# Batch 0 of a Fourier-filter and MLP kernel: one spectrum for both filter products, a second inverse table for the factor i, angles by integer shifts, input DMAs first

## Chip, cores, metric

One core of a Trainium2 chip. The metric is the device time of one execution in microseconds (us). Most executions of one kernel agree within 0.3%. Every quoted ratio is the mean time of one kernel's fast runs over that of the kernel before in the same rounds on the same chip, so it is not quite the ratio of the medians quoted beside it; the brackets hold a 95% interval. Medians of different kernels come from different rounds and chips; so where a gain in us is given, it is the excess of a median over that of the kernel before in the same rounds.

## The reference, cut to what matters

```python
# x: (8, 3008, 256), filt_r and filt_i: (1505, 256), w_in: (256, 2048), w_out: (2048, 256)
X = np.fft.rfft(x, axis=1)
Y = X * (filt_r + 1j * filt_i)[None]
y = np.fft.irfft(Y, n=3008, axis=1).reshape(24064, 256)
h = y @ w_in
return (0.5 * h * (1 + erf(h / sqrt(2)))) @ w_out
```

## The kernel before

The transforms are matmuls with tables of sines. Batch 0 goes first, alone; the MLP follows, with batches 1 to 7 woven between its matmuls. Only batch 0's prologue matters here. A filter product (`c2`) multiplies the spectrum by `filt_r` and by `filt_i`. The second product needs the spectrum turned by i, so PE computes it twice, from a table `T2` that holds three forms of each row side by side (turned with a minus, plain, turned):

```python
# c2: filter product p of 12 (two of 24 frequency rows)
for t, o in ((0, 1), (1, 0)):
    for i in range(2):
        k = 2 * p + i
        nc.tensor.matmul(ps[:, t, 256 * i:256 * i + 256],
                         lhsT=self.T2[:, k, o:o + 2].rearrange("p a b -> p (a b)"),
                         rhs=self.st[0, "b", k // 4][:, k % 4, :], start=True, stop=True)
f = self.F[:, :, 2 * p:2 * p + 2, :]
nc.vector.tensor_tensor(out=w, in0=ps, in1=f.rearrange("p t a b -> p t (a b)"), op=ALU.mult)   # VectorE
# c3: inverse transform; t = 0 and t = 1 add up in PSUM, both with the same table
nc.tensor.matmul(ps[half][:, c:c + 128], lhsT=w[:, t, o:o + 128],
                 rhs=self.T3[:, 2 * (p + i) + k]..., start=t == 0, stop=t == 1)
```

The filter `F` is loaded to partitions 0 to 63 and must also stand in 64 to 127. The order of what touches it (cuts marked):

```python
m.load_x(0, 1, 4)                                      # x: casting DMAs from GpSimd
...
for k, n in ((0, 4), (4, 4), (8, 8), (16, 8)):
    m.load_filters(k, n)                               # 16 casting DMAs from GpSimd
m.dup_filters(nc.gpsimd, 4, 4)                         # copies to partitions 64 to 127, two rows each
m.load_w_in()
m.dup_filters(nc.gpsimd, 8, 8)
...                                                    # column transforms c1, c1t
m.dup_filters(nc.vector, 0, 4)
...
m.dup_filters(nc.gpsimd, 16, 8)
m.load_x(1); m.load_w_out(0); m.load_w_out(8)
m.c2(0); m.c2(1)
...                                                    # q = 1 to 6: c2, c1t, c3; table_4 at q = 4
# the tail: c3t (transposes) and c4 (last transform), then the MLP with batch 1's first step s1 in slot 1
```

Of the kernel before, what the change touches and what calls it, by code (L numbers as in the profile page):

```python
# [21 lines left out]
TCH = 512  # L22

# [5 lines left out]
class _Mix:  # L29
    def __init__(self, ctx, tc, x, filt_r, filt_i, w_in, w_out, out):  # L30
# [23 lines left out]
        self.T2 = c.tile([128, K1, 3, NB], BF16, name="T2")  # L54
# [42 lines left out]

    def gate(self, t):

        g = self.po.tile([1, 1], BF16, tag="gate", name="gate")  # L100
        self.nc.gpsimd.tensor_copy(out=g, in_=t)  # L101
# [22 lines left out]
    def table_1(self, g):  # L124
# [3 lines left out]
        k48 = self.iota(g, "k48", [128, 2, K1], [[0, 2], [1, K1]])  # L128
        off = g.tile([128, 2, K1], FP32, name="off")
        nc.gpsimd.memset(off[:, 0, :], 0.25)  # L130
        nc.gpsimd.memset(off[:, 1, :], 0.5)
# [7 lines left out]
        nc.vector.scalar_tensor_tensor(out=w, in0=k48, scalar=n1, in1=off, op0=ALU.mult, op1=ALU.add)  # L139
# [6 lines left out]
    def table_2(self, g):  # L146
# [8 lines left out]
        self.n2, ri = col("n2"), col("ri")  # L155
        v.tensor_copy(out=self.n2, in_=m_i)
        v.tensor_copy(out=ri, in_=ri_i)
        ts(out=self.n2, in0=self.n2, scalar1=1.0 / self.S, scalar2=None, op0=ALU.mult)
        ts(out=ri, in0=ri, scalar1=-0.25, scalar2=0.25, op0=ALU.mult, op1=ALU.add)
        self.jn = g.tile([128, NB], FP32, name="jn")  # L160
        ts(out=self.jn, in0=self.jj, scalar1=self.n2, scalar2=ri, op0=ALU.mult, op1=ALU.add)
        self.n12, self.sg, self.to = col("n12"), col("sg"), col("to")
        ts(out=self.n12, in0=self.n2, scalar1=float(K1 // 2), scalar2=None, op0=ALU.mult)

        ts(out=self.sg, in0=ri, scalar1=8.0, scalar2=-1.0, op0=ALU.mult, op1=ALU.add)
        v.tensor_tensor(out=self.to, in0=self.p, in1=self.sg, op=ALU.add)

    def unit_matrices(self, g, cols):
        ts = self.nc.vector.tensor_scalar
        self.eye, self.swap = (g.tile([128, 128], BF16, name=n) for n in ("eye", "swap"))  # L170
        ts(out=self.eye, in0=cols, scalar1=self.p, scalar2=None, op0=ALU.is_equal)
        ts(out=self.swap, in0=cols, scalar1=self.to, scalar2=self.sg, op0=ALU.is_equal, op1=ALU.mult)

    def table_2_angle(self, h):

        v, k = self.nc.vector, K1 // 2
        w, r = self.gen[:, h], self.gen[:, 2]
        if h == 0:
            v.scalar_tensor_tensor(out=w, in0=self.kk.unsqueeze(2).to_broadcast([128, k, NB]), scalar=self.n2,
                                   in1=self.jn.unsqueeze(1).to_broadcast([128, k, NB]), op0=ALU.mult, op1=ALU.add)  # L180
        else:
            v.tensor_scalar(out=w, in0=self.gen[:, 0], scalar1=self.n12, scalar2=None, op0=ALU.add)
        v.tensor_scalar(out=r, in0=w, scalar1=RND, scalar2=-RND, op0=ALU.add, op1=ALU.add)
        v.tensor_tensor(out=w, in0=w, in1=r, op=ALU.subtract)

    def table_2_sin(self, h):
        self.nc.scalar.activation(out=self.T2[:, 12 * h:12 * h + 12, 1, :], in_=self.gen[:, h], func=AF.Sin,
                                  scale=2.0 * PI)

    def table_2_swap(self, h):  # L190
        t2 = self.T2[:, 12 * h:12 * h + 12]
        for i in range(2):
            ps = self.bank("ps_sw", "n")
            self.nc.tensor.matmul(ps[:, 0:384], lhsT=self.swap, rhs=t2[:, :, 1, 32 * i:32 * i + 32],
                                  start=True, stop=True)
            self._evac(t2[:, :, 2, 32 * i:32 * i + 32], ps[:, 0:384].rearrange("p (k j) -> p k j", k=12),
                       "act", 1.0 - 2.0 * i)
            if h == 1:
                self._evac(t2[:, :, 0, 32 * i:32 * i + 32], ps[:, 0:384].rearrange("p (k j) -> p k j", k=12),
                           "act", 2.0 * i - 1.0)  # L200

    def table_2_minus(self):
        t2 = self.T2[:, 0:12]
        self.nc.vector.tensor_scalar(out=t2[:, :, 0, :], in0=t2[:, :, 2, :], scalar1=-1.0, scalar2=None, op0=ALU.mult)
# [22 lines left out]
    def table_3(self, q, eng):  # L227
        ps = self.bank("ps_t3", "n", BF16)
        for i in range(8):
            self.nc.tensor.transpose(ps[:, 128 * i:128 * i + 128],  # L230
                                     self.T2[:, 8 * q + i, 1:3].rearrange("p a b -> p (a b)"), self.eye)

        self._evac(self.T3[:, 8 * q:8 * q + 8], ps.rearrange("p (k n r) -> p k r n", k=8, r=2), eng)

    def warm_up(self, n):

        ps = self.bank("ps_warm", "w")
        for i in range(n):
            self.nc.tensor.matmul(ps[:, i % 2], lhsT=self.ones[:, 0:128], rhs=self.ones, start=True, stop=True)
# [50 lines left out]
    def s2(self, b, p):  # L290
        nc = self.nc
        ps = self.bank("ps_s2")
        for i in range(2):
            k = 2 * p + i
            nc.tensor.matmul(ps[:, 256 * i:256 * i + 256], lhsT=self.T2[:, k, 1:3].rearrange("p a b -> p (a b)"),  # L295
# [70 lines left out]
    def c1t(self, q, eng):  # L366
# [6 lines left out]
        self._evac(b[:, 0:4, :].rearrange("p a b -> p (a b)"), ps, eng)  # L373

    def c2(self, p):
# [4 lines left out]
        for t, o in ((0, 1), (1, 0)):  # L380
            for i in range(2):
                k = 2 * p + i
                nc.tensor.matmul(ps[:, t, 256 * i:256 * i + 256],
                                 lhsT=self.T2[:, k, o:o + 2].rearrange("p a b -> p (a b)"),
                                 rhs=self.st[0, "b", k // 4][:, k % 4, :], start=True, stop=True)
# [121 lines left out]
def kernel(  # L507
# [50 lines left out]
    for u in range(16):  # L558
# [9 lines left out]
        if u == 11:  # L568
            m.warm_up(2)
# [115 lines left out]
```

## Time and profile before

The median is 774.5 us. The stages, from the busy time by stage that the prediction quotes (span 772.2 us):

| stage | us | what sets it |
|---|---|---|
| loads of x and filter, tables, column transforms | 0 to 16.72 | the load of x |
| 12 filter products | 16.72 to 32.02 | VectorE, then GpSimd's copies of F |
| tail: inverse transform to y | 32.02 to 40.55 | VectorE's copies and ACT's evictions in turn |
| first MLP tile, with batch 1's first step | 40.55 to 50.92 | PE, busy 10.33 of 10.37 us |
| the rest | 721.28 long | PE, busy 718.32 us |

### The profile page before, as it was taken

To read this page: it belongs to the slowest core of one execution; us is meant where nothing else is said; L and a number is where in the kernel's file an instruction comes from. 1 tells how busy PE (TensorE), PEld (TensorE's weight loads), DVE (VectorE), ACT (ScalarE), POOL (GpSimd) and SP (SyncE) were. 2 spreads that over 40 slices of the span, in tenths; PEclk is the share of its full clock that TensorE was granted. 3 is DMA by queue.
4 is the path that set the end of the run, shared out by engine and by line. 5 is a ranking of instruction groups with operands and counts; after the bars stand their busy time and mean duration, and the time that the engine had idled before them with its cause. 6 is when DMAs were issued, how large, how long until landed. Compare 5 with 4: busy or idle time off the path is not lost.

```text
span 772.2 us, 15059 instructions
## 1 busy us (share of the span) xinstructions
PE 763.2 (99%) x6066; PEld 528.7 (68%) x6066; DVE 397.3 (51%) x722; ACT 567.4 (73%) x981; POOL 64.9 (8%) x160
## 2 busy tenths in 40 slices
PE   8999999999999999999999999999999999999998
PEld 4847675676776766677777776666776776766666
DVE  7866755464555645457463664637646366411011
ACT  6879955897568975699656996579865798666663
POOL 7801100020000200011000110001100000000000
PEclk9999999999999999999999999999999999999999
DMA  8894745466253661636516464255553422410111
GB/s 138 145 180 124 150 123 129 128 124 151 57 139 107 138 159 41 192 78 122 143 53 181 85 133 123 79 154 95 124 137 81 139 83 69 123 42 28 42 42 55
DMA packets 87398, 85.66 MB, mean 111 GB/s; under 512 B 6752, under 2 KB 77536, under 8 KB 87328
## 3 DMA queue, kind: packets, MB, share of 16 engines
q1 hardware_dynamic: 78816, 68.70, 31.0%
q0 software_dynamic: 8512, 16.00, 14.9%
q8 instruction: 47, 0.77, 0.4%
q14 instruction: 23, 0.19, 0.1%
HBM read 54.00 MB, written 46.66 MB: 130 GB/s over the span
## 4 chain that ended last, share of the span: by engine, by line
PE 94%; DMA 3%; POOL 2%; issue 0%; DVE 0%; POOLq 0%
PE ps_o L488 43%; PE ps_h L461 42%; PE ps_s L345 2%; PE ps_s L320 2%; PE ps_s L295 2%; PE ps_s L272 2%; DMA x_sb<-in_x_dram 2%; POOL F L96 1%; POOL x_sb L82 1%; DMA F<-in_filt_i_dram 1%; POOL F L91 0%; PE ps_e L478 0%; POOL T1s L258 0%; DVE ost L501 0%; POOL T1p L580 0%
## 5 line engine op out<-in xcount | busy, mean ns | idle before, releaser
L464 ACT ACTIVATE g_sb<-ps_h 128x512 bf16<-128x512 f32 x752 | 438.0, 597 | 182.8 <-PE ps_h L461 172.1
L488 PE MATMUL ps_o<-w_out_sb,g_sb 128*128 128x256 bf16 x2992 | 447.5, 273 | 0.0
L461 PE MATMUL ps_h<-y_sb,w_in_sb 128*128 128x512 bf16 (+3 forms) x1600 | 445.8, 366 | 0.7 <-DMA x_sb<-in_x_dram 0.7
L488 PEld LDWEIGHTS <-g_sb 128*128 128x128 bf16 x2992 | 283.9, 98 | 134.3 <-issue 9.9
L461 PEld LDWEIGHTS <-w_in_sb 128*128 128x128 bf16 x1600 | 154.7, 98 | 23.7 <-issue 1.1
L494 DVE COPY ost<-ps_o 128x512 f32<-128x512 f32 x93 | 63.8, 686 | 143.5 <-PE ps_o L488 143.4
L303 DVE TENSOR_TENSOR p<-ps_s,F 128x512 bf16<-128x512 f32 x84 | 58.1, 691 | 105.9 <-ACT p L302 89.5
L249 DVE TENSOR_SCALAR y_sb<-ps_s 128x376 bf16<-128x376 f32 x112 | 60.9, 548 | 80.5 <-PE ps_s L345 80.5
L247 DVE CAST a_sb<-ps_s 128x512 bf16<-128x512 f32 x112 | 69.3, 682 | 27.7 <-PE ps_s L272 27.7
L247 DVE CAST v_sb<-ps_s 128x512 bf16<-128x512 f32 x84 | 57.4, 684 | 2.9 <-PE ps_s L320 2.6
L301 ACT ACTIVATE p<-ps_s 64x512 bf16<-64x512 f32 x84 | 49.9, 594 | 2.1
L302 ACT CAST p<-ps_s 64x512 bf16<-64x512 f32 x84 | 48.5, 577 | 1.0
L345 PEld LDWEIGHTS <-d_sb 96*128 96x128 bf16 x448 | 30.8, 97 | 25.3 <-DMA d_sb<-R 0.2
L101 POOL COPY gate<-p 1x1 bf16<-1x1 bf16 x48 | 8.5, 178 | 470.3 <-DVE p L305 470.3
L305 DVE TENSOR_TENSOR p<-p 128x512 bf16<-128x512 bf16 x84 | 35.7, 425 | 2.9
L345 PE MATMUL ps_s<-T,d_sb 96*128 96x94 bf16 x448 | 36.3, 204 | 0.0
L304 DVE TENSOR_TENSOR p<-p,F 128x512 bf16<-128x512 bf16 x84 | 34.8, 415 | 0.0
L82 POOL DMA_DIRECT2D x_sb<-in_x_dram x64 | 32.7, 512 | 13.0 <-issue 12.5
L320 PE MATMUL ps_s<-p,T 128*128 128x256 bf16 x168 | 32.1, 273 | 0.0
L295 PE MATMUL ps_s<-b_sb,T 128*128 128x256 bf16 x168 | 32.1, 273 | 0.0
L320 PEld LDWEIGHTS <-T 128*128 128x128 bf16 x168 | 16.4, 98 | 20.1 <-DVE p L305 0.5
L295 PEld LDWEIGHTS <-T 128*128 128x128 bf16 x168 | 16.4, 98 | 13.4
(103 smaller groups left out, 189.1 us busy)
## 6 DMA issues: line engine op xcount, KB each, us to landing
out_dram<-ost SPq DMA_DIRECT2D x93, 256.0 KB, 2.3
x_sb<-in_x_dram POOLq DMA_DIRECT2D x64, 188.0 KB, 3.8
R<-a_sb SPq DMA_DIRECT2D x112, 96.0 KB, 2.1
b_sb<-R SPq DMA_DIRECT2D x28, 384.0 KB, 4.3
R<-v_sb SPq DMA_DIRECT2D x42, 256.0 KB, 3.5
d_sb<-R SPq DMA_DIRECT2D x56, 192.0 KB, 4.7
w_in_sb<-in_moe_w_in_dram POOLq DMA_DIRECT2D x2, 512.0 KB, 7.8
w_out_sb<-in_moe_w_out_dram POOLq DMA_DIRECT2D x2, 512.0 KB, 11.3
```

What stands on the lines that cost most here:

```text
L247: self.nc.vector.tensor_copy(out=out, in_=in_)
L249: self.nc.vector.tensor_scalar(out=out, in0=in_, scalar1=scale, scalar2=None, op0=ALU.mult)
L295: nc.tensor.matmul(ps[:, 256 * i:256 * i + 256], lhsT=self.T2[:, k, 1:3].rearrange("p a b -> p (a b)"), rhs=self.st[b, "b", k // 6][:, k % ...
L301: nc.scalar.activation(out=p2[0:64], in_=ps[64:128], func=AF.Copy, scale=-1.0)
L302: nc.scalar.copy(out=p2[64:128], in_=ps[0:64])
L303: nc.vector.tensor_tensor(out=p1, in0=ps, in1=f(0), op=ALU.mult)
L320: nc.tensor.matmul(ps[:, 256 * i:256 * i + 256], lhsT=self.T3[:, k].rearrange("p a b -> p (a b)"), rhs=w[:, 256 * i:256 * i + 256], start= ...
L345: nc.tensor.matmul(ps[:, 94 * i:94 * i + 94], lhsT=d[:, (grp % 2) * 4 + i, 128 * half:128 * half + 128], rhs=t4, start=True, stop=True)
L461: nc.tensor.matmul(ps[:, o:o + n], lhsT=self.w_in_sb[:, dc, jc * 128:jc * 128 + 128], rhs=self.ring[:, dc, off:off + n], start=(dc == 0), ...
L464: nc.scalar.activation(out=self.st["g", t][:, jc, :], in_=ps, func=AF.Gelu)
L488: nc.tensor.matmul(ps[:, tile_i % 2, :], lhsT=g[:, jc, tile_i * 128:tile_i * 128 + 128], rhs=self.w_out_sb[:, jc, :], start=(jc == 0), sto ...
L494: nc.vector.tensor_copy(out=ost, in_=ps)
```

## The change

Its intent: PE computes the spectrum once, and VectorE reads it twice through a stride of zero. The factor i moves into a second inverse table `T3i`, which GpSimd makes from `T3` by swapping halves and multiplying by a sign for each partition. Angles are reduced by an integer shift instead of rounding. The first x DMA goes ahead of the iotas. To make room on GpSimd, 14 of the 24 rows of F are copied by DMA from SyncE's queue, and the loads of w_in, of batch 1's x and of w_out move behind the filter work. The core of the diff (cut: the tables' angles and signs, the new tile shapes, PSUM pools, the order of set-up, which engine evicts what, the eviction of `c1t(0)` in two pieces, and the making of `T1q`, which goes from ACT to GpSimd):

```diff
 # c2
-for t, o in ((0, 1), (1, 0)):
-    for i in range(2):
-        k = 2 * p + i
-        nc.tensor.matmul(ps[:, t, 256 * i:256 * i + 256], lhsT=self.T2[:, k, o:o + 2]...
+for i in range(2):
+    k = 2 * p + i
+    nc.tensor.matmul(ps[:, 256 * i:256 * i + 256], lhsT=self.T2[:, k]...
-    nc.vector.tensor_tensor(out=w, in0=ps, in1=f..., op=ALU.mult)
+    nc.vector.tensor_tensor(out=w, in0=ps.unsqueeze(1).to_broadcast([128, 2, 512]), in1=f..., op=ALU.mult)
 # c3
-    rhs=self.T3[:, 2 * (p + i) + k]...
+    rhs=(self.T3i if t else self.T3)[:, 2 * (p + i) + k]...
 # table_3, called for q = 0, 1, 2
+    for r in range(2):
+        self.nc.gpsimd.tensor_scalar(out=self.T3i[:, k, r, :], in0=self.T3[:, k, 1 - r, :],
+                                     scalar1=self.turn[r], scalar2=None, op0=ALU.mult)
+def dup_filters_dma(self, k0, k):
+    self.nc.sync.dma_start(out=self.F[64:128, :, k0:k0 + k, :], in_=self.F[0:64, :, k0:k0 + k, :])
 # order
-m.p = m.iota(g, "p", ...)
-m.load_x(0, 0, 1, (0,))
+m.load_x(0, 0, 1)
+m.p = m.iota(g, "p", ...)
-for k, n in ((0, 4), (4, 4), (8, 8), (16, 8)): m.load_filters(k, n)
-m.dup_filters(nc.gpsimd, 4, 4); m.load_w_in(); m.dup_filters(nc.gpsimd, 8, 8)
+m.load_filters(0, 4); m.load_filters(4, 4)
 ...                                     # column transforms; after: table_3(0) with its two T3i here
+m.load_filters(8, 8); m.load_filters(16, 8)
+m.dup_filters_dma(2, 2); m.dup_filters_dma(4, 4)
-m.dup_filters(nc.vector, 0, 4)
+m.dup_filters(nc.vector, 0, 2)
 m.c2(0); m.c2(1)
+m.table_3(1)                            # the second pair of T3i
+m.dup_filters(nc.gpsimd, 8, 8); m.dup_filters_dma(16, 8)
-m.dup_filters(nc.gpsimd, 16, 8); m.load_x(1); m.load_w_out(0); m.load_w_out(8)
 ...                                     # q = 1 to 6
+    if q == 3: m.table_3(2); m.load_w_in(); m.load_x(1); m.load_w_out(0); m.load_w_out(8)
-    if q == 4: m.table_4(m.T4c, m.T1q, m.wtc)
 ...
+m.weights_4(g); m.table_4(m.T4c, m.T1q, m.wtc)
+nc.scalar.activation(out=warm, in_=m.p, func=AF.Gelu)        # was ahead of c1t
-s1, ... = 1, 4, 16, 26, ...             # batch 1's first step
+s1, ... = 0, 4, 15, 25, ...             # now before the first MLP matmul
```

## The prediction

> **What bounds the kernel now.** I first read the busy shares of the page, then the busy time by stage, with cuts at the starts of groups that I took from the order of time.
>
> ```profile
> PE 763.2 (99%) x6066; PEld 528.7 (68%) x6066; DVE 397.3 (51%) x722; ACT 567.4 (73%) x981; POOL 64.9 (8%) x160
> ...
> 0.00:16.72 16.72, 12.90 (x110) 7.30 (x111) 12.93 (x42) 10.63 (x20) 12.85 (x35) 1.00 0.86 139
> 16.72:32.02 15.30, 14.51 (x194) 12.64 (x191) 14.00 (x13) 14.11 (x26) 14.94 (x23) 1.00 0.80 127
> 32.02:40.55 8.53, 7.11 (x132) 6.66 (x133) 6.74 (x12) 6.04 (x17) 4.18 (x8) 1.00 1.02 182
> 40.55:50.92 10.37, 10.33 (x64) 3.71 (x65) 9.05 (x15) 7.45 (x15) 0.00 (x0) 1.00 1.07 188
> 50.92:772.20 721.28, 718.32 (x5570) 498.43 (x5568) 354.61 (x642) 529.20 (x907) 32.95 (x96) 1.00 0.43 108
> ```
>
> The columns after the length are PE, PEld, DVE, ACT, POOL, granted clock and DMA. From 50.92 us on, PE works 718.3 of 721.3 us at full clock, with the two matrices of the MLP and batches 1 to 7 woven in. The filter of batch 0 is a prologue that ends at 40.55 us, where the MLP starts; nothing but this prologue is rewritten (for batches 1 to 7 the forward table only has another layout, and batch 1's first step moves by one slot). So the whole change is worth at most what it does to those 40.55 us, and 2% of 774.5 is 15.5 us. The prologue would have to lose 38% for "faster".
>
> Inside the prologue I read each engine in order of time. VectorE first: it carries the middle and the tail.
>
> ```profile
> 16.72 4.82 DVE L388 TENSOR_TENSOR p<-ps_c,F 128x1024 bf16<-128x1024 f32 x4
> 22.43 6.88 DVE L388 TENSOR_TENSOR p<-ps_c,F 128x1024 bf16<-128x1024 f32 x6 [0.88 <-POOL F L96]
> 29.61 1.23 DVE L388 TENSOR_TENSOR p<-ps_c,F 128x1024 bf16<-128x1024 f32 x1 [0.30 <-POOL F L96]
> 30.75 1.27 DVE L392 TENSOR_TENSOR p<-ps_c,F 128x512 bf16<-128x512 f32 x2
> ...
> 33.69 5.56 DVE L247 COPY d_sb<-ps_c3t 96x1024 bf16<-96x1024 bf16 x8 [0.75 <-PE ps_c3t L424]
> 39.23 1.17 DVE L249 TENSOR_SCALAR y_sb<-ps_c 128x376 bf16<-128x376 f32 x2
> ```
>
> The 12 filter products run nearly back to back from 16.72 to 32.02 us, and the copies of d from 33.69 to 39.25. The two waits inside are for GpSimd, which copies the filter to the lower 64 partitions. GpSimd and the input transfers before it:
>
> ```profile
> 1.33 0.69 POOL L82 DMA_DIRECT2D x_sb<-in_x_dram  x1 [0.37 <-issue]
> ...
> 13.23 0.55 POOL L91 DMA_DIRECT2D F<-in_filt_i_dram  x1 [0.38 <-DMA x_sb<-in_x_dram]
> 13.78 1.08 POOL L91 DMA_DIRECT2D F<-in_filt_r_dram  x2
> ...
> 18.12 2.02 POOL L96 COPY F<-F 64x1024 bf16<-64x1024 bf16 x2
> 20.09 1.11 POOL L111 DMA_DIRECT2D w_in_sb<-in_moe_w_in_dram  x2
> 21.36 7.93 POOL L96 COPY F<-F 64x1024 bf16<-64x1024 bf16 x8 [0.15 <-DMA F<-in_filt_i_dram]
> ```
>
> The chain that ended last says the same: from 5.88 to 12.95 us it lies on the load of x, from 15.36 to 21.23 on the load of the filter, then on GpSimd's copies.
>
> **What the Trainium skill says.** "VectorE: DVE Perf Modes", section "The perf-mode tier table", has tensor_tensor with a PSUM operand at 1x, at 0.96 GHz: 1024 / 0.96 = 1.07 us. The trace agrees: 1.215 us each, 1.13 to 1.2 from start to start. Reading one spectrum twice through a stride of zero therefore gives VectorE nothing; it still writes 1024 elements. "GPSIMD Engine Reference", section 3.1, gives bodies of one or two operations about 1.03 cycles an element at 1.2 GHz. The trace's 1024-element copies take 1.04 us, 1.22 cycles. "DMA: Bandwidth & Descriptors", section "SWDGE vs HWDGE vs iDMA", says that a casting DMA must come from GpSimd; x and the filter are cast, so they stay there at 0.51 to 0.55 us of issue each, while the new plain copies F to F can go through SP. "ScalarE: Activation LUTs", section "What ACT_TABLE_LOAD costs", has 1283 ns for a table load plus 1380 ns of drain; this trace has the 1.28 us at 14.51, but the next activation starts 0.02 us after it, so I count 1.3.
>
> **The change part by part.**
>
> *One spectrum.* 24 matmuls of 256 columns go (4 per pair become 2; a group of 4 takes 0.44 us from start to next start, so 0.22 us a pair, 2.6 us of PE). PE is not the bound there: it waits for VectorE's products. Worth 0 on the path. The third copy of the table goes with its 2 ACT evictions (0.8 us) and one VectorE instruction (0.35 us), all beside other work.
>
> *Angles by shifts.* VectorE drops 1.01+0.56+0.96+0.61+0.56+0.96 = 4.66 us between 5.75 and 10.92 for an estimated 0.55+0.35+0.56+0.61+0.56 = 2.6 us (halves and equals of those rows). But this stretch waits for x: PE stands 1.25 us until a DMA at 9.38 us, and at 13.09 again. So only slack.
>
> *Inputs first.* The first x issue comes before two iotas instead of after: I take 1.0 instead of 1.33 us. The load is limited by DMA (about 200 GB/s from 6 us on), so the last piece lands about 0.4 us earlier, 12.55 for 12.95. Column transforms end at 13.95 (was 14.5), c1t's eviction is cut in two, and VectorE copies 2 of 4 filter rows itself (0.42 for 0.78 us): the first product starts at about 15.85 instead of 16.72 us.
>
> *Factor i in a second table.* GpSimd gets six tensor_scalars of 512 elements, by its copy's rate an estimated 0.6 us each, in program order before the next filter loads and before its filter copies. I walk it: last x landed 12.55; issue of the last of the first eight filter loads to 13.4; T1q, T1p, T1s, memset (about 0.27+0.27+0.14+0.48+0.1) to 14.65; first two table instructions to 15.9; eight issues of 0.54 to 20.2; two more table instructions to 21.4; copy of filter rows 8 and 9 to 22.5. Before, that copy came at 22.4. So product 4 starts at about 22.5 us again, although product 3 is done at 20.6: the head start of 0.87 us is eaten, and a wait of about 2 us on GpSimd appears. The copies then come every 1.04 us, faster than products. Rows 16 to 23 come by DMA: filter loads issued from 15.9 to 20.2 land near 23.8 (before, 13.78 to 18.07 landed at 21.23), and half a MB from SBUF to SBUF takes an estimated 3.5 us (256 KB stores take 2.3): 27.3, where product 8 wants it at 27.2. Seven more starts of 1.13 and the last pair of 1.27 after product 4 give an end near 32.1 us: the same as before.
>
> *Tail.* The Gelu table load moves from 14.51, where it delayed one eviction, to just ahead of the y evictions. ACT must wait for the weights (four small VectorE instructions, now after the last v eviction), then 0.35 + 1.28 + 0.2: its first y eviction comes about 0.4 us later than 2.85 us after the last product. 14 of them at 0.39 end 0.35 us later than now. Against that batch 1's first step (8 matmuls, 0.56 us) now stands before the first MLP matmul and fills the wait for the last y: it needs only banks free by the second to last eviction. Net about 0.3 us gained.
>
> *Moved loads.* w_in is issued at about 27 instead of 20.1, x of batch 1 at 28 to 36, w_out at 36 to 38 instead of 34.2. 3.6 MB at about 195 GB/s after 27.5 end at 46 to 49 us; the first use of w_out is at about 50.6. It just fits.
>
> Sum: 0 to +0.2 in the products, -0.3 in the tail: -0.2 us, 774.3.
>
> **Rivals.** (1) GpSimd's table instructions or loads are quicker than I think and product 4 does not wait: then the 0.87 us and the old 1.18 us of waits are won, the products end near 30.0, and with the tail 772.2. For it: GpSimd's parts are the roughest durations on the page, and such an order looks chosen from a trace. Against it: the 4.3 us of filter issues now follow work that itself waits for x. (2) The table instructions take 1 us each, or the F-to-F transfers queue behind the loads on the same DMA engines (share 0.8 to 1.0 in this stretch): 4 times 0.4 us before product 4, or 1 to 2 at product 8: 775.5. (3) w_out lands late and the first second-matrix matmul waits: up to 2 us more, 776; for it only the tight margin of 2 us. (4) A matmul bound: if PE carried the products, 2.6 us would be won; against it, PE has waits on VectorE between the groups in that stretch.
>
> **Range and chances.** The sum says 774.3; rival 1 seems likelier to me than 2 and 3 together, which pulls it to 773.8. Low is rival 1 whole, 772.2, high 775.3. 2% cannot be reached by a prologue of 40.55 us in which the loads, 12 products of 1.13 us (13.6) and a tail of 8.5 us stay: faster 0.01, same 0.98, slower 0.01.
>
> **What would show it.** Right: first filter product near 15.9 us; a wait of 1 to 2.5 us on GpSimd's F copy before the fifth product, at 22 to 23 us; last product ending at 31.5 to 32.5; ACT's table load just before y evictions; first MLP matmul of slot 1 near 41.4 us (41.7 now); the stretch from there to the end equal within 0.5 us. Wrong: no such wait (rival 1), a wait on the DMA for rows 16 to 23 or for rows 2 to 7 (rival 2), a PE wait on w_out near 51 us (rival 3), or a different length of the stretch after the MLP starts, which I hold for fixed.

## The result, and the profile after

The kernel after takes 783.46 us (782.85 to 784.15, 4 runs) beside 774.54 us of the kernel before (774.31 to 775.08, 4 runs): ratio 1.0114 [1.0097, 1.0132]. The result is correct. Less than 2% was right; the time was 9.7 us above the 773.8 predicted and well outside the range.

Busy shares of the page of after, and its busy time by stage with cuts at the same five marks (columns as in the prediction: PE, PEld, DVE, ACT, POOL, granted clock, DMA):

```profile
PE 762.2 (97%) x6039; PEld 527.1 (67%) x6039; DVE 397.4 (51%) x730; ACT 565.8 (72%) x975; POOL 68.3 (9%) x159
...
17.13:37.18 20.05, 13.50 (x162) 11.70 (x159) 14.01 (x13) 12.57 (x22) 18.92 (x23) 0.83 0.63 100
37.18:47.29 10.11, 7.87 (x141) 6.87 (x142) 7.21 (x16) 7.59 (x18) 4.43 (x8) 1.00 1.08 204
47.29:59.24 11.95, 9.88 (x61) 3.63 (x57) 8.98 (x15) 7.51 (x15) 0.00 (x0) 1.00 1.26 218
59.24:782.30 723.06, 718.82 (x5570) 498.17 (x5568) 354.88 (x642) 529.05 (x907) 32.77 (x96) 1.00 0.43 107
```

PE does 1.0 us less work over the span, and only GpSimd does much more (3.4 us): what has grown is waits. The page alone does not say where; the stages do. From first product to last took 15.30 us before and takes 20.05; VectorE's 14.0 us of work in it is unchanged, and GpSimd is busy 18.92 of the 20.05. With the five marks, the profiled 10.1 us add up as: first product 0.41 later, products +4.75, tail +1.58, first MLP tile +1.58, the rest +1.78.

VectorE of after in order of time (start, duration, engine, line, operation; in brackets the idle time ahead and what ended it):

```profile
17.13 2.35 DVE L407 TENSOR_TENSOR p<-ps_c,F 128x1024 bf16<-128x1024 f32 x2
20.77 2.36 DVE L407 TENSOR_TENSOR p<-ps_c,F 128x1024 bf16<-128x1024 f32 x2 [1.28 <-PE ps_c L424]
27.60 4.62 DVE L407 TENSOR_TENSOR p<-ps_c,F 128x1024 bf16<-128x1024 f32 x4 [4.48 <-POOL F L97]
...
57.63 2.48 DVE L266 CAST a_sb<-ps_s 128x512 bf16<-128x512 f32 x4 [2.75 <-DMA R<-a_sb]
```

The predicted wait before the fifth product is there and ends on the predicted copy, but it is 4.48 us instead of about 2, and the fifth product starts at 27.60 instead of 22.5. From there the products take 9.58 us to the end, as before (9.59). The last line is new: VectorE waits in the first MLP tile for a store of batch 1's first step to leave its buffer. Before, the same casts ran without such a wait:

```profile
46.74 4.87 DVE L247 CAST a_sb<-ps_s 128x512 bf16<-128x512 f32 x8 [0.29 <-PE ps_s L272]
```

The 1.28 us ahead of the third product are put down to PE by the profile, but the matmuls that it needs were done near 19.2 us. The copy of F rows 4 to 7 by DMA landed at 20.64, 0.13 us before the product starts, and in e1, e2, e7 and e8 the third product also starts 0.12 to 0.13 us after this copy lands. So this wait is for F by DMA; the longer wait at the fifth product hides it.

GpSimd of after, and the pieces of its chain of work that ended last:

```profile
15.80 1.70 POOL L251 TENSOR_SCALAR T3i<-T,turn_r 128x512 bf16<-128x512 bf16 x1
17.49 1.55 POOL L251 TENSOR_SCALAR T3i<-T,turn_i 128x512 bf16<-128x512 bf16 x1
19.00 1.14 POOL L92 DMA_DIRECT2D F<-in_filt_r_dram  x2
...
23.37 1.57 POOL L251 TENSOR_SCALAR T3i<-T,turn_r 128x512 bf16<-128x512 bf16 x1
24.92 1.55 POOL L251 TENSOR_SCALAR T3i<-T,turn_i 128x512 bf16<-128x512 bf16 x1
26.54 3.98 POOL L97 COPY F<-F 64x1024 bf16<-64x1024 bf16 x4
...
34.60 1.14 POOL L115 DMA_DIRECT2D w_in_sb<-in_moe_w_in_dram  x2
...
43.81 0.92 POOL L119 DMA_DIRECT2D w_out_sb<-in_moe_w_out_dram  x1 [0.78 <-DMA x_sb<-in_x_dram]
```

```profile
15.80 3.24 POOL T3i L251 x2
19.04 4.30 POOL F L92 x8
...
50.61 6.91 DMA R<-a_sb
```

The chain shows the walk of the prediction, order and all. What is not as predicted is the length of a table instruction: 1.55 to 1.70 us for 512 elements, where 0.6 was assumed. The loads of w_in and w_out, pushed on by this, are issued at 34.6 and 43.8 us instead of 27 and 36; at 50.6 the chain lies for 6.91 us on a store of 96 KB. In the DMA view from 13 to 60 us the stores of batch 1's first step take twice as long from issue to landing as before; first before, then after (count, KB each, median us):

```profile
R<-a_sb SPq DMA_DIRECT2D x16, 96.0 KB, 2.6
```

```profile
R<-a_sb SPq DMA_DIRECT2D x13, 96.0 KB, 5.8
```

In the tail, PE's first transposes wait for a bank (PE in order of time):

```profile
39.10 1.50 PE L440 MATMUL ps_c3t<-eye,vt_sb 128*128 128x128 bf16 x24 [1.43 <-ACT T4c L264]
```

That is 1.92 us after the last product; before, it was 0.97:

```profile
32.99 1.50 PE L424 MATMUL ps_c3t<-eye,vt_sb 128*128 128x128 bf16 x24 [0.52 <-DVE vt_sb L247]
```
The eviction of the small table `T4c`, now last in the filter stage, holds the bank that the first transpose takes over.

### The profile page after: what moved, and what is told of

Read it like the earlier page. It is cut to its first block, busy times and chain, and to the rows that moved or that the text cites. A ratio compares the mean times of both kernels' runs of the same rounds, so it can differ in the third digit from the quotient of the medians.

```text
span 782.3 us, 15017 instructions
## 1 busy us (share of the span) xinstructions
PE 762.2 (97%) x6039; PEld 527.1 (67%) x6039; DVE 397.4 (51%) x730; ACT 565.8 (72%) x975; POOL 68.3 (9%) x159
## 4 chain that ended last, share of the span: by engine, by line
PE 91%; DMA 4%; POOL 2%; DVE 1%; issue 1%; SPq 0%; ACT 0%; POOLq 0%; DVEq 0%; ACTq 0%
PE ps_o L504 41%; PE ps_h L477 40%; PE ps_s L364 2%; PE ps_s L314 2%; PE ps_s L339 2%; PE ps_s L291 2%; DMA d_sb<-R 2%; DMA x_sb<-in_x_dram 1%; DMA R<-a_sb 1%; POOL T3i L251 1%; POOL F L92 1%; DMA R<-v_sb 1%; PE ps_c3t L440 0%; POOL x_sb L83 0%; DVE p L407 0%
## 5 line engine op out<-in xcount | busy, mean ns | idle before, releaser
L477 PEld LDWEIGHTS <-w_in_sb 128*128 128x128 bf16 x1600 | 154.8, 98 | 25.5 <-issue 3.7
```

The source lines that it names most:

```text
L477: nc.tensor.matmul(ps[:, o:o + n], lhsT=self.w_in_sb[:, dc, jc * 128:jc * 128 + 128], rhs=self.ring[:, dc, off:off + n], start=(dc == 0), ...
```

## The experiments

My theory after reading the traces: the main loss is GpSimd's multiplication, one term of the prediction's sum (A). Rivals or additions: the F copies by DMA (B), the tail's order (C), loads that come late into the MLP (D), the granted clock, 0.83 in the product stage (E). Inputs first and the single spectrum were to be tested for the gain that they should have brought (F). Eighteen kernels ran and one did not build. Each row is a median, its ratio to before, and five marks of its one profiled execution: start of the first and fifth filter product, end of the last, then the tail and first MLP tile together (end of products to first second-matrix matmul), then the rest. The two are added because batch 1's first step, moved by the change, shifts 0.56 us from one to the other.

| kernel | median us | ratio | 1st | 5th | end | tail + tile | rest |
|---|---|---|---|---|---|---|---|
| before | 774.5 | 1 | 16.72 | 22.43 | 32.02 | 18.90 | 721.28 |
| after | 783.5 | 1.0114 [1.0097, 1.0132] | 17.13 | 27.60 | 37.18 | 22.06 | 723.06 |
| e1 | 779.8 | 1.0080 [1.0054, 1.0106] | 18.26 | 24.59 | 34.47 | 19.84 | 722.29 |
| e2 | 782.8 | 1.0114 [1.0099, 1.0129] | 16.38 | 26.89 | 37.66 | 19.84 | 723.30 |
| e3 | 782.1 | 1.0105 [1.0090, 1.0121] | 17.51 | 27.42 | 36.62 | 22.23 | 721.45 |
| e5 | 780.7, one run | none | 16.62 | 25.72 | 35.73 | 21.06 | 722.11 |
| e6 | 773.9 | 1.0000 [0.9986, 1.0013] | 16.56 | 22.12 | 31.73 | 18.90 | 721.57 |
| e7 | 783.9 | 1.0121 [1.0104, 1.0138] | 17.43 | 27.33 | 37.97 | 20.60 | 723.83 |
| e8 | 779.9 | 1.0078 [1.0064, 1.0091] | 16.52 | 25.46 | 35.55 | 21.24 | 721.81 |
| e9 | 777.0 | 1.0040 [1.0028, 1.0053] | 17.65 | 24.83 | 34.38 | 18.88 | 721.44 |
| e10 | 777.3 | 1.0045 [1.0032, 1.0059] | 16.94 | 23.11 | 32.84 | 18.88 | 721.78 |
| e11b | 775.3 | 1.0016 [1.0001, 1.0030] | 17.57 | 22.42 | 32.42 | 19.78 | 721.30 |
| e12 | 778.4 | 1.0072 [1.0044, 1.0100] | 17.79 | 24.51 | 34.32 | 18.87 | 722.71 |
| e13 | 780.3 | 1.0080 [1.0067, 1.0093] | 16.77 | 26.84 | 38.18 | 18.99 | 721.33 |
| e14 | 778.1 | 1.0042 [1.0027, 1.0057] | 17.24 | 22.81 | 35.02 | 19.42 | 723.16 |
| e15 | 779.9 | 1.0069 [1.0053, 1.0085] | 16.24 | 21.20 | 31.21 | 24.39 | 721.40 |
| e16 | 773.4 | 0.9989 [0.9976, 1.0001] | 18.00 | 22.88 | 32.89 | 18.87 | 721.14 |
| e17 | 775.6 | 1.0022 [1.0010, 1.0034] | 17.36 | 22.20 | 31.41 | 20.01 | 722.28 |
| e18 | 781.5, two groups | 1.0101 [1.0062, 1.0140] | 17.69 | 31.68 | 41.72 | 18.87 | 723.31 |
| e19 | 779.2 | 1.0060 [1.0045, 1.0074] | 18.35 | 23.32 | 33.32 | 22.06 | 723.42 |

The start of the first product varies from 16.2 to 18.4 us, also between kernels that have the same code up to there, so differences of a microsecond in one profile's marks are noise unless a wait shows them. e5, e8, e14 and e17 are wrong; all others are correct.

### A. The multiplication on GpSimd

**e5** puts a copy, a multiplication by a constant and one by the partition's scalar side by side on GpSimd, in place of the six table instructions (wrong result):

```diff
+if q == 0 and r == 0 or q == 2 and r == 1:
+    self.nc.gpsimd.tensor_copy(out=o, in_=i)
+elif q == 0 and r == 1 or q == 2 and r == 0:
+    self.nc.gpsimd.tensor_scalar(out=o, in0=i, scalar1=-1.0, scalar2=None, op0=ALU.mult)
+else:
+    self.nc.gpsimd.tensor_scalar(out=o, in0=i, scalar1=self.turn[r], scalar2=None, op0=ALU.mult)
```

> Wrong result on purpose; measures the disputed cost. Of the six 512-element table instructions on GpSimd two become plain copies, two take a constant for the factor, two keep the per-partition factor. If the per-partition scalar is what makes them slow: copy 0.55 us, constant 0.6, per-partition 1.55. If multiplying at all is slow there: copy 0.55, the others both 1.55. If the strided 8x64 pattern is slow: all three near 1.5 us.

GpSimd in order of time, e5:

```profile
15.03 0.61 POOL L253 COPY T3i<-T 128x512 bf16<-128x512 bf16 x1
15.62 1.51 POOL L255 TENSOR_SCALAR T3i<-T 128x512 bf16<-128x512 bf16 x1
...
21.48 1.58 POOL L257 TENSOR_SCALAR T3i<-T,turn_r 128x512 bf16<-128x512 bf16 x1
```

The copy of this shape is indeed 0.61 us, as the prediction worked out from other copies. It is multiplying that costs two and a half times that, and a scalar from memory hardly adds to it.

**e8** makes all six table instructions plain copies (wrong result), so that the prediction's assumed 0.6 us holds:

```diff
-self.nc.gpsimd.tensor_scalar(out=self.T3i[:, k, r, :], in0=self.T3[:, k, 1 - r, :], scalar1=self.turn[r], ...)
+self.nc.gpsimd.tensor_copy(out=self.T3i[:, k, r, :], in_=self.T3[:, k, 1 - r, :])
```

> The changed kernel with the six multiplications on GpSimd replaced by copies of the same shape, measured at 0.61 us in e5 (1.55 before): they now cost what my prediction took. Wrong result on purpose. Theory G: the fifth product starts 4 times 0.94 us earlier, near 23.8 us; products end near 33.4; w_in is issued near 29, the stall in the first MLP tile is gone; the time falls by 3.8 + 2.4 to about 777.2. If theory G is not the main cause: over 780. What stays above 774.5 is then x, tail and later waits.

The time falls by 2.7 us, from an excess of 8.9 to one of 6.2 us (ratio 1.0114 to 1.0078, intervals apart). That is between the two forecasts, so the multiplication is a cause, but not most of the loss. The fifth product comes at 25.46, not at the 22.5 of the prediction, because another wait has stepped in at the third (VectorE in order of time, e8):

```profile
23.19 6.88 DVE L406 TENSOR_TENSOR p<-ps_c,F 128x1024 bf16<-128x1024 f32 x6 [4.32 <-DMA F<-in_filt_r_dram]
```

GpSimd no longer stands in the way of the fifth product, and the wait is for filter rows that come by DMA. The profile names a load, but the loads of rows 4 to 7 had landed by 16.90 us; their copy by DMA, issued at 16.98, landed at 23.07. So the mis-sized term is worth about 2.7 us of time and hid a second bound right behind it.

**e1** gives the six instructions to VectorE, with the correct result:

```diff
-self.nc.gpsimd.tensor_scalar(out=self.T3i[:, k, r, :], ...
+self.nc.vector.tensor_scalar(out=self.T3i[:, k, r, :], ...
```

> The six tensor_scalar instructions that make the second inverse table run on VectorE instead of GpSimd (the result stays right). Theory G (the 1.55 us instructions on GpSimd, in program order before the filter copies, are the cause, and the late weight and x loads follow from them): the filter loads for rows 8 to 23 are issued from about 15.8 us (19.0 in the changed kernel), the copy of rows 8 and 9 ends near 22, the fifth product starts near 22.2 us (27.6), the products end near 32.5 (37.2), the 2.1 us wait on the a stores after 50 us is gone; time 775 to 777. Theory C (PE fell to a lower clock in its 4.4 us pause and that is what costs) and theory D (the copies inside the core's memory and the loads share the DMA engines, so the filter arrives late anyway): fifth product not before 25.5 us, time over 780. VectorE pays six instructions of an estimated 0.25 us.

VectorE needs 0.35 us for what takes GpSimd 1.55:

```profile
20.75 0.35 DVE L251 TENSOR_SCALAR T3i<-T,turn_r 128x512 bf16<-128x512 bf16 x1
```

The excess is 6.0 us, 2.9 less than after and much as in e8; the runs spread from 778.2 to 782.65, and the interval touches that of after. The profiled one is among the fast ones. Both forecasts missed: the fifth product comes at 24.59, between 22.2 and 25.5. Here too the third product waits (0.95 us) for the copy of rows 4 to 7, which lands at 22.19, 0.13 us ahead of it.

### B. The F copies by DMA

**e13** puts only this part of the change, without rows 2 and 3, into the kernel before:

```diff
-m.dup_filters(nc.gpsimd, 4, 4)
+m.dup_filters_dma(4, 4)
-m.dup_filters(nc.gpsimd, 16, 8)
+m.dup_filters_dma(16, 8)
```

> The kernel before with one part of the change alone: filter rows 4 to 7 and 16 to 23 are copied by DMA instead of GpSimd. Theory D2: rows 4 to 7 take 6 us instead of the 2.0 us of two GpSimd copies, the third product waits until 22 to 23 us (19.1 before), products end 1 to 3 us later: 775 to 777. If copies by DMA are harmless by themselves: 773.0 to 774.0, as the two waits on GpSimd (1.2 us) go.

The third product waits 5.29 us. VectorE in order of time, then the two copies in the DMA view (from issue to landing), e13:

```profile
24.42 3.63 DVE L391 TENSOR_TENSOR p<-ps_c,F 128x1024 bf16<-128x1024 f32 x3 [5.29 <-DMA F<-F]
```

```profile
F<-F SPq DMA_DIRECT2D x1, 256.0 KB, 6.9
...
F<-F SPq DMA_DIRECT2D x1, 512.0 KB, 8.8
```

The same two transfers in after:

```profile
F<-F SPq DMA_DIRECT2D x1, 512.0 KB, 4.4
F<-F SPq DMA_DIRECT2D x1, 256.0 KB, 3.0
```

In after they are quick because the filter loads that would compete come late, held up by the multiplications. When loads are in flight at the same time they take twice as long. The Trainium skill, "DMA: Bandwidth & Descriptors", section "Queues, rings and completion order", has each DMA engine take packets from its queues in turn, so that a copy on an own queue still shares the engines; the 3.0 against 6.9 us agree. Alone in the kernel before, this part costs 6.4 us by the medians of its rounds (780.28 and 773.85), more than forecast. Part of that may come from GpSimd having less to do: it issues w_in 1.9 us and batch 1's x 4.8 us earlier (18.17 for 20.09, 25.37 for 30.19), and these loads compete with the copies too.

**e9** and **e10** keep the change and order it otherwise: all filter loads early as in the kernel before, w_in right behind the F copies (24.5 and 24.7 us, where after has 34.6), GpSimd copying F rows 4 to 15, DMA for rows 2, 3 and 16 to 23, the Gelu table and `table_4` early, and `T3i` made by ACT (first third), VectorE (second) and GpSimd in e9 or VectorE in e10 (third):

```diff
+for k, n in ((0, 4), (4, 4), (8, 8), (16, 8)):
+    m.load_filters(k, n)
+m.dup_filters_dma(2, 2); m.dup_filters(nc.gpsimd, 4, 4); m.dup_filters(nc.gpsimd, 8, 8)
+m.dup_filters_dma(16, 8); m.load_w_in()
 ...
+    if u == 11: m.turn_3(0, act)
+m.turn_3(1, nc.vector)
-            m.turn_3(2, nc.gpsimd)      # e9
+            m.turn_3(2, nc.vector)      # e10
```

> A mended version, result right: all filter loads issued at once as in the kernel before, the second inverse table made by ACT (first third), VectorE (second) and GpSimd after the w_in loads (last), rows 4 to 15 of the filter copied by GpSimd, rows 2, 3, 16 to 23 by DMA, last table's weights and Gelu table load early again. If the one-spectrum form has any gain to give: no wait at the fifth product, first product near 16.6, products end near 31 us, time 772.8 to 773.8. If its gain is nothing because VectorE's 12 products set the pace: 774 to 775.

> As e9, with the last third of the table on VectorE too: 0.7 us more there, x and w_out of the main stage issued 3.1 us earlier. Products end 0.5 to 0.7 us later than in e9; if the late loads still cost something in e9, the time is equal or lower, else 0.5 us higher.

Both come to 777: 3.3 and 3.5 us above before, where after has 8.9. Tail and first tile cost as much as before the change (18.88). The second product waits 0.70 and 1.02 us for rows 2 and 3 by DMA (128 KB, 4.9 us from issue to landing, where after has 3.4). e10's profiled run, at 775.33 us, is the fastest of its five (up to 778.22), so its marks explain less than the median's 3.5 us.

**e12** takes the DMA copies out of e10: VectorE copies rows 0 to 3 and GpSimd 4 to 23, with w_in between them, as in the kernel before.

```diff
-m.dup_filters_dma(2, 2)
 m.dup_filters(nc.gpsimd, 4, 4)
+m.load_w_in()
 m.dup_filters(nc.gpsimd, 8, 8)
-m.dup_filters_dma(16, 8); m.load_w_in()
+m.dup_filters(nc.gpsimd, 16, 8)
-m.dup_filters(nc.vector, 0, 2)
+m.dup_filters(nc.vector, 0, 4)
```

> As e10, but all filter rows are copied as in the kernel before (0 to 3 by VectorE, 4 to 23 by GpSimd), none by DMA. Theory D2 (once GpSimd is freed, the copies by DMA are the next limit, because they queue behind the filter loads on the same engines: 6.1 to 6.3 us for 256 KB in e1 and e8, 3.0 when the loads came later): the wait at the second product (0.7 to 1.0 us in e9 and e10) is gone, products end near 32.3 us, and the runs lie within 1.5 us of each other: 773.5 to 774.5. If the spread of e10 (775.3 to 778.2) and its later time have another cause: 776 to 778 again.

It is not faster (1.0072; five runs from 777.6 to 779.6 and one of 785.68). No product waits for a DMA, but VectorE's table instructions take 0.99 and 1.12 us where e10 has 0.34 and 0.35. **e18** mends a fault that e14 (below) had shown, `T1q` made behind GpSimd's copies:

```diff
-nc.gpsimd.tensor_copy(out=m.T1q, in_=m.T1...)
 m.c1t(1, act)
+nc.scalar.copy(out=m.T1q, in_=m.T1...)
```

> e12 with the same mending, result right: one spectrum, the second table by ACT (first third) and VectorE (the rest), filter copied without DMA. Against e17 this shows the price of the second table off GpSimd: 4 instructions of 0.35 to 1.1 us on VectorE, which is the pace-setter. Expected 1.5 to 2.8 us above e17: products end at 33.5 to 34.5 us, time 776 to 777.5; if VectorE had slack, equal to e17 within 0.5.

Its six runs fall into two groups, 777.1 to 778.0 and 785.0 to 786.5 us; the granted clock doesn't part them (0.996 is in both). The fast group lies 3.3 to 4.2 us above its kernel before, no better than e9 and e10. The profile fell in the slow one and shows why (VectorE, then GpSimd, in order of time):

```profile
20.35 0.35 DVE L258 TENSOR_SCALAR T3i<-T,turn_r 128x512 bf16<-128x512 bf16 x1 [0.30 <-ACT T L270]
20.62 8.88 DVE L258 TENSOR_SCALAR T3i<-T,turn_i 128x512 bf16<-128x512 bf16 x1
```

```profile
21.44 7.91 POOL L97 COPY F<-F 64x1024 bf16<-64x1024 bf16 x8
```

The same instruction, 0.35 us before it, lasts 8.88 us and ends when GpSimd's eight copies end. The Trainium skill, "SBUF — State Buffer", section "Who interferes with whom", has a port pair that either VectorE in its two-port modes or GpSimd holds for a whole instruction, while the other is blocked. The times agree with such a lock (the lock itself is no row of a trace); what is new is that VectorE would have lost it to eight instructions in a row. The trace doesn't show why it didn't come first: its row begins 0.8 us before the first copy, while GpSimd still issues the loads of w_in. That the other two runs of 785 and 786 us, and e12's of 785.68, had the same is inferred from their times: they have no profile. So in the orders tried neither way of copying F left room for VectorE to make `T3i`: by DMA the copies collide with loads, on GpSimd with VectorE's own table work.

### C. The order of the tail

**e7** puts `weights_4` and `table_4` back to their early places:

```diff
+m.weights_4(g)
 m.table_2_rows(g)
 ...
+        if q == 4: m.table_4(m.T4c, m.T1q, m.wtc)
 ...
-m.weights_4(g)
-m.table_4(m.T4c, m.T1q, m.wtc)
```

> The weights and the transpose for the last table go back to where the kernel before has them (weights at the start, transpose in the fifth step of the products); the Gelu table load stays late. Reading of the trace: in the changed kernel the first transposes of v wait 1.43 us for ACT's eviction of that table, because they take the bank that it frees. Expected: they start 0.97 us after the last product as before, not 1.92, and the time falls by 0.6 to 0.9 us to 782.5 to 782.9. If the late Gelu load sets the y evictions anyway: under 0.3 us.

The first transpose follows 0.96 us after the last product again, and the tail is 0.97 us shorter than in e1 and e2, which keep the late table (9.37 against 10.34 us). The time did not fall: 1.0121. In the profile two products wait 1.47 and 1.34 us for F by DMA, and the rest is 0.8 us longer than after. What the late Gelu load leaves is small: 9.37 us against 9.15 in e9, e10 and e16, where it is early. So the tail's loss is shown as a cost in its own stage, and not as time of the kernel.

**e16** puts batch 1's first step ahead of the first MLP matmul in the kernel before, with the PSUM split that it needs:

```diff
-s1, n1, r1, s2, n2, r2, s4, n4 = 1, 4, 16, 26, 2.8, 61, 68, 0.72
+s1, n1, r1, s2, n2, r2, s4, n4 = 0, 4, 15, 25, 2.8, 61, 68, 0.72
-m.psum(wide, v=(5, 1), t=(3, 1))
+m.psum(wide, v=(4, 1), t=(4, 1))
```

> The kernel before with one part of the change alone: batch 1's steps one slot earlier, so that its first 8 matmuls stand before the first MLP matmul, and the last stage's banks 4 and 4 instead of 5 and 3. My prediction's tail term says 0.3 us gained: 773.5 for 773.85. If the order is worth nothing: 773.85 within 0.2.

Tail and tile together 18.87 instead of 18.90, ratio 0.9989 [0.9976, 1.0001]: nothing, or a tenth of a per cent. It is the only ratio below 1, and not clearly; no version beats both kernels beyond doubt.

### D. Loads that come late

**e2** gives only the last third of `T3i` to VectorE, so w_in and x are issued 4.9 us and w_out 2.9 us earlier, and nothing else:

```diff
-self.nc.gpsimd.tensor_scalar(
+(self.nc.vector if q == 2 else self.nc.gpsimd).tensor_scalar(
```

> Only the third pair of the table (needed late) moves to VectorE. The fifth product stays at 27.6 us and the products end at 37.2 as in the changed kernel, but GpSimd issues the w_in, x and w_out loads right after its last filter copy, at about 30.6 us instead of 34.6. Theory G with its second part (the loads that are late collide with the stores of batch 1's first step and stall the first MLP tile by 2.3 us): that stall shrinks to under 1 us, time 780.5 to 781.8. If the stall has another cause (the stores are slow whenever w_out is loading): the time stays at 783.4 within 0.6.

The stall is gone: tail and tile 19.84 for 22.06. But w_in now shares the engines with the F copies, a product waits 0.94 us for F by DMA, and in the rest PE waits 1.3 us and its weight loads 1.7 us on `d_sb<-R`; the time is that of after (1.0114). **e11** was to delay w_out alone in the kernel before, by GpSimd work in its own buffer; SBUF had no room for the buffer, so it did not build and did not run. **e11b** does it in place:

```diff
 m.load_x(1)
+for _ in range(2):
+    nc.gpsimd.tensor_scalar(out=m.ones, in0=m.ones, scalar1=1.0, scalar2=None, op0=ALU.mult)
 m.load_w_out(0)
```

> The kernel before with two idle multiplications (3.0 us) on GpSimd between the loads of x and of w_out, so that w_out is issued 3.3 us ahead of the first MLP matmul, as in the changed kernel (3.5), not 6.3; the prologue ends at 40.55 us as ever. Theory (late loads collide with the stores of batch 1's first step): the first MLP tile takes 11.9 us and not 10.37, with a wait of VectorE on the stores of a; time 776 to 777. If the stall of the changed kernel has another cause: 774.5 within 0.5.

> As e11, which did not build: the kernel before with two multiplications (3.0 us) that change nothing on GpSimd between the loads of x and of w_out, so that w_out is issued some 3.3 us ahead of the first MLP matmul (3.5 in the changed kernel, 6.3 before). Theory (late loads collide with the stores of batch 1's first step): the first MLP tile takes near 11.9 us and not 10.37, with a wait of VectorE on the stores of a; time 775.5 to 777. If the stall of the changed kernel has another cause: 773.8 within 0.5.

w_out is 3 us later, nobody waits for a store, and the tile is 10.37 us, as before. One late load is not enough. (The tail is 0.9 us longer because the memset of `vt` comes later on GpSimd too.) **e15** and **e19** delay all three loads in the kernel before:

```diff
 m.dup_filters(nc.gpsimd, 4, 4)
-m.load_w_in()
 m.dup_filters(nc.gpsimd, 8, 8)
 ...
 m.dup_filters(nc.gpsimd, 16, 8)
 ...
+m.vt = ...; nc.gpsimd.memset(m.vt[:, :, 96, :], 0.0)     # e19 only: was after the loads, in c3t
+m.load_w_in()
 m.load_x(1)
 m.load_w_out(0)
```

> The kernel before with the load of w_in moved behind the filter copies (issued near 30 us, not 20), just ahead of x and w_out, as the changed kernel has it; nothing else moves. Theory (late loads together collide with the stores of batch 1's first step): the last two x loads wait for w_in, w_out is issued at 38 to 41 us, the first MLP tile takes 11.5 to 13 us and not 10.37, with a wait of VectorE or PE on the stores of a or on loads; time 775.5 to 777.5. If the stall of the changed kernel needs something else: 773.8 within 0.6.

> e15 mended: there the memset of v's last columns stood behind the late loads on GpSimd and the tail waited 3.4 us for it; now it is made ahead of them. The kernel before with w_in, x and w_out all issued after the filter copies. Theory (late loads collide with the stores of batch 1's first step): end of products and tail as before or 0.5 us earlier, the first MLP tile takes 11.3 to 13 us and not 10.37; time 774.5 to 776.5. If late loads are harmless: 10.37 again and 773.3 to 774.2.

e15 was spoiled, more than e11b: the memset of `vt` came to stand behind the loads on GpSimd, and PE waited 3.4 us for it. e19 mends that and has the stall of after in the kernel before, larger (VectorE in order of time, e19):

```profile
54.21 2.48 DVE L247 CAST a_sb<-ps_s 128x512 bf16<-128x512 f32 x4 [3.69 <-DMA R<-a_sb]
```

Its tile is 13.54 us for 10.37 and its time 1.0060. So it is shown in this pair of kernels that late loads can make the first MLP tile wait (the profiled run is the slowest of e19's four, which begin at 777.1 us). It takes more than lateness, though: e17 (section F) waits 1.66 us with w_out issued at 34.27 us, as in the kernel before (34.22).

Which transfer holds up a store was not tested. The landings point to w_out: wherever batch 1's first stores are issued with w_out still in flight and no store is waited for by more than 0.3 us (before and ten variants), the first store lands 0.2 to 0.4 us after the second half of w_out, 47.56 after 47.26 us in the kernel before. Where the tile stalls by more than a microsecond (after, e3, e7, e17, e19), the stores land some 0.4 to 1.6 us apart until w_out has landed (59.79 in after) and 0.2 to 0.3 us apart just behind it.

### E. The clock

In after PE is idle 4.42 us before 28.88, and the granted clock of the product stage is 0.83. **e3** fills the gap with matmuls nobody uses:

```diff
+if q == 3:
+    gap = m.bank("ps_gap", "n")
+    for _ in range(20):
+        nc.tensor.matmul(gap, lhsT=m.ones[:, 0:128], rhs=m.ones, start=True, stop=True)
 m.c2(2 * q + 1)
```

> 20 matmuls on ones (about 4.3 us) fill the pause of PE before the eighth spectrum. Theory C: the clock stays at 1.00 from 17 to 37 us and the products end earlier by 1 to 2 us, time near 782. Theory G: the clock stays at 1.00 and nothing else moves, because VectorE's products set the pace after the pause (9.58 us from the fifth product to the end against 9.59 in the kernel before): time 783.4 within 0.6.

The granted clock of the product stage (17.51 to 36.62 us) is then 1.00, and from fifth product to end it takes 9.20 us for 9.58. The median is what theory C expected, but its rounds were faster: the excess is 8.3 us where after has 8.9, and the ratios' intervals overlap widely. So the low clock follows from the wait, and what it costs, some 0.7 us, isn't clear of noise; VectorE and not PE carries the products.

### F. The expected gains

**e6** issues the first two x DMAs ahead of the iotas in the kernel before:

```diff
-m.p = m.iota(g, "p", [128, 1], [[0, 1]], cm=1)
-m.load_x(0, 0, 1, (0,))
+m.load_x(0, 0, 1)
+m.p = m.iota(g, "p", [128, 1], [[0, 1]], cm=1)
 m.pi = m.iota(g, "pi", [128, 1], [[0, 1]], cm=1, dt=I32)
-m.load_x(0, 0, 1, (1,))
```

> The kernel before with one part of the change alone: the first two x loads are issued ahead of the two iotas. My prediction's step: first issue 0.3 us earlier, last piece of x lands 0.4 us earlier than 12.95 us, first product near 16.3, time 774.1. The trace of the changed kernel says otherwise (first issue at 1.22 for 1.33, last x piece near 13.5): then first product 16.7 to 17.1 and the time 774.5 to 775.0.

Ratio 1.0000. The first issue moves from 1.33 to 1.24 us only: without the iota ahead of it, GpSimd sits 0.80 us before its first DMA instead of 0.37.

**e14** and **e17** remove the second table altogether, from e12's order (wrong result), which leaves the single spectrum with the copies as in the kernel before:

```diff
-rhs=(self.T3i if t else self.T3)[:, 2 * (p + i) + k]...
+rhs=self.T3[:, 2 * (p + i) + k]...
-m.turn_3(0, act) / m.turn_3(1, nc.vector) / m.turn_3(2, nc.vector)
-nc.gpsimd.tensor_copy(out=m.T1q, ...)                  # e17 only
+nc.scalar.copy(out=m.T1q, ...)                         # e17 only
```

> Wrong result on purpose: e12 without the second inverse table (both halves of the sum take the first one), so the one-spectrum form at no cost for the factor i, with the filter copied as in the kernel before. If the saved matmuls and evictions of the one-spectrum form are worth anything by themselves: products end near 30.5 us, time 772.3 to 773.2. If VectorE's 12 products and GpSimd's filter copies set the pace in any case, as my prediction said: products end at 31.5 to 32.5 us, time 773.5 to 774.5.

> e14 mended: there GpSimd made T1q only behind its filter copies, and PE waited 3.3 us for it; now ACT makes it, as in the kernel before. Wrong result on purpose: one spectrum, no second table. If the one-spectrum form has a gain of its own: products end before 31 us, time 772.3 to 773.3. If VectorE's products and the filter copies set the pace: first product near 17, products end at 31.9 to 32.6, time 773.8 to 775.

e14 was spoiled: `T1q`, on GpSimd behind its copies, held PE for 3.3 us. e17 is clean in the products: first to last in 14.05 us with 0.22 us of wait, which is VectorE's pace and 1.25 us less than before. Some of that is only its later start: kernels of the old form whose first product comes as late (e11b, e16, e19) take 14.85 to 14.97 us, so 0.8 to 0.9 us are left for the single spectrum, in one profile each. Yet its time is 1.0022: the profile loses the gain again to 1.7 us on `R<-a_sb` in the first tile and 1.3 us on `d_sb<-R` later. The single spectrum, free of every cost of its second table, wins nothing that reaches the end in this order; whether it would without the wait on the stores is not shown.

## Why the prediction was wrong, step by step

- **Bound and ceiling: right.** Only the prologue and what it leaves behind moved; 2% was not reached in either direction. (The "lower 64 partitions" of the prediction are partitions 64 to 127.)
- **One spectrum, worth 0: right.** PE has waits in that stretch before and after, VectorE's product is 1.215 us with the zero stride as without, and e17 shows no gain in time, though its products are up to 0.9 us quicker.
- **Angles by shifts, only slack: not tested alone.** In after the chain still lies on the load of x from 5.90 to 13.58 us, so a shorter VectorE stretch there could not show. The five instructions take 2.76 us, where 2.6 were estimated.
- **Inputs first, first product at 15.85: wrong.** x landed at 13.58, not 12.55, and the first product came at 17.13; with the same code up to there, e2, e3, e5 and e8 have 12.81 to 13.35 and 16.38 to 17.51, so x varies by 0.8 us, but is never as early as predicted. e6 shows no gain from the order itself (its interval, 1 us to either side, could hide the 0.4 expected); the issue moved by 0.09 us there, not by the 0.33 assumed.
- **Factor i in a second table, "an estimated 0.6 us each": the step that failed.** The order walked was right, and so was the wait it names; the term was mis-sized. It measured 1.55 to 1.70 us (e5: it is the multiplication), the four ahead of the copy of rows 8 and 9 take 6.35 us where 2.4 were counted: 3.95 of the 5.1 us by which the fifth product is late, and x, landed 1.03 us late, is nearly all of the rest. In time it is 2.7 to 2.9 us of the 8.9 (e8, e1). The prediction took a copy's rate for an arithmetic instruction, and where the page that it names gives several rates in its section 3.1, from 1.03 cycles for the simplest bodies to 2.6 for two inputs, it quoted only the lowest.
- **F to F by DMA, 3.5 us, just in time: right in after, for the wrong reason.** 4.4 us for rows 16 to 23, and nobody waited for it, since all else was late. The third product did wait 1.28 us for rows 4 to 7, which the prediction left out of its walk. With loads in flight the two copies take 6.9 and 8.8 us (e13), as rival 2 feared. They are a second bound behind the first: that is why e1 and e8 win no more in the products.
- **Products' pace after the fifth: right.** 9.58 us, predicted 9.6. (The sum as written, seven starts of 1.13 and a pair of 1.27, is 9.2; e3, which has no wait there, took 9.20, and after has one of 0.27.)
- **Rivals.** Rival 1, no wait, was the one I leaned to, and it was wrong. Rival 2 had the direction, both its parts and one of its signs (the wait for rows 4 to 7), but 1 us for a table instruction was still too low, and it counted the parts one at a time.
- **Tail, 0.3 us gained: wrong.** +1.58 us, 0.56 of it moved out of the next stage by the order of batch 1's step. I had looked at ACT's evictions and not at which bank `T4c` occupies; PE waits 1.43 us for it. The order of batch 1's step gains nothing in tail and tile (e16: 18.87 for 18.90 us).
- **Moved loads, "It just fits": wrong, and not where rival 3 looked.** No matmul waits for w_out. The loads, issued 7 to 8 us later than I had worked out, slow the stores of batch 1's first step, and the first tile waits for those: +1.58 us, or 3.16 together with the tail, of which e2 (loads earlier) gives back 2.2 in this stage, though not in the time.
- **The stretch after the MLP's start, "equal within 0.5 us": wrong.** It is 1.8 us longer in the profiled run even after the first tile. Waits on `d_sb<-R` make up about 2 us of PE and its weight loads. e3 and e9, with 721.4, have under 0.8; e2 has 3.0, and e7 has as much as after and 2.1 on `b_sb<-R` besides.

What stays open: the part of those later waits that the change makes necessarily (they move from run to run), why e10's median is 2 us above its profiled run, through which transfer the late loads hold up a store (the landings point to w_out, no run tests it), and why e17 has that wait with its loads on time.

So of the 8.9 us, some 2.8 are GpSimd's multiplication; another 2.7 went with loads, tables and tail put back in order (e9, e10); the last 3.4 us did not come back in any correct variant that keeps the second table, and their cause is open.

## What to carry to other kernels

Before work moves to another engine, find in the trace the same operation on that engine, not another one of the same shape: here a multiplication cost 2.5 times a copy. When an order is bound by one engine, ask what the next wait in line would be, since taking off the first one wins only the distance to the second. And a load "that just fits" has to be held against all the transfers that run with it, small stores above all, and not only against its own first use.

## What the Trainium skill lacked or had wrong

- "GPSIMD Engine Reference", section 3.1: no row for a multiplication by a scalar in bf16. Its 1.03 cycles for bodies of one or two operations would be 0.44 us for 512 elements at its 1.2 GHz; a copy took 0.61 us and a multiplication 1.51 us by a constant, 1.55 to 1.70 by a scalar for each partition. With its fixed part that is 3.5 to 4.0 cycles an element, above the section's 1.03, 1.8 and 2.6. For copies the 1.03 holds: those of 512 and of 1024 elements, 0.61 and 1.04 us, differ by 1.0 cycle an element.
- "SBUF — State Buffer", section "Who interferes with whom": says that the loser of the port pair is blocked until the other's instruction ends. In e18 a VectorE instruction of 0.35 us lasted 8.88 us beside eight GpSimd copies in a row; the page does not say that the loser may lose again and again.
- "DMA: Bandwidth & Descriptors", section "Queues, rings and completion order": the turn-taking is there, the price is not. 256 KB from SBUF to SBUF took 3.0 us with the loads out of the way and 6.9 us beside them.
- "ScalarE: Activation LUTs", section "What ACT_TABLE_LOAD costs": the 1380 ns of drain are not seen here either. In after the load starts at 39.07 and takes 1.28 us, and the next activation starts at 40.36.
